# In-projection of three of six chunks: the seven-product scheme applied twice, with 49 products of 128 columns

## The chip, the cores and the metric

The kernel runs on one core of a Trainium2 chip. The metric is the device time of one execution in microseconds. Engines: PE (TensorE, matmuls), PEld (its weight loads), DVE (VectorE), ACT (ScalarE), POOL (GpSimd), SP (SyncE, which issues nearly all DMAs). Each engine runs its own queue in order and waits on semaphores for the others.

## The reference

Attention with a mask by clusters over 4 x 8 heads of 768 tokens, then two projections with a gate between them, on 3072 tokens:

```python
x = attn_out.transpose(0, 2, 1, 3).reshape(B * S, H * D)   # 3072 x 512
h = x @ w_in                                               # w_in 512 x 2048
sp = np.maximum(h, 0.0) + np.log1p(np.exp(-np.abs(h)))     # softplus
g = h * erf(sp)
return (g @ w_out).astype(np.float32)                      # w_out 2048 x 512
```

Everything here is in float32. The change concerns `x @ w_in` and the gate behind it.

## The kernel before

The first 408 us are the attention. Then the 3072 tokens run in six chunks of 512 (`CT`), each an in-projection, a gate and an out-projection.

**The seven-product scheme.** A product of two matrices cut into 2 x 2 blocks is made from seven block products instead of eight, at the price of sums of blocks before (`left_forms`, `right_forms`) and after. `lefts` and `rights` name the seven left and right operands by number: 1, 2 and 3 to 7, some of them blocks as they are, some of them sums (`new[0]`, `new[1]`, `new[2]` and one block that is overwritten).

**In-projection before.** The scheme is applied once: x in two halves of tokens (256 columns, `HT`) and two of rows, w_in in halves of rows and columns. `hidden` (called by `hidden26` for chunks 1 to 5, once for each `lot`) goes over four blocks of 128 hidden columns. `block` makes the seven products in the order 1, 2, 6, 7, 5, 3, 4, each of two matmuls of 128x128 weights by 256 columns in a PSUM bank, and after each product its additions out of PSUM (`fresh`): product 1 is copied by ACT, the others are added by DVE into the tiles `g`. So an in-projection is 2 lots x 4 blocks x 7 products x 2 = 112 matmuls. Between the products, one piece of other work at a time is taken off `aside_work`: the gate of the lot before (softplus and erf on ACT, then products on DVE) and the sums that the out-projection needs. The eight PSUM banks are used in turn.

**Out-projection before.** `project26` has 26 products of four matmuls of 256 columns (`RIGHT`, `LEFT`), with sums of blocks of g on DVE between them (`LEFT_STEPS`, each with the product p behind which it stands), and additions and copies out of PSUM on DVE and ACT (`AFTER`, one product behind). Ten of the right operands are streamed from DRAM into three places (`ring`, `load_stream`), issued by SP after the matmuls that used the place. The last quarter of the gate (lot 1, half 1) is done at its start: `curves` for p = −1, 0, 1, 2 on ACT and four gate products on DVE at p = 4 and 5. In its last four products DVE makes the x sums for the next chunk, and SP loads x two chunks ahead at p = 12.

**Order.** All instructions of PE, DVE, ACT and POOL are kept in the order in which the program gives them (`InOrder`); the order is written out by hand. Tiles come from pools: `gp` (g, four), `actp` (one buffer `a_s` for softplus and erf), `outp` (two, the output), `xp` (two, x). A tile that is asked for again waits until its last reader is done. `extra` are the spare rooms in the tiles that hold the ring.

```python
ORDER = (1, 2, 6, 7, 5, 3, 4)
```

Of the kernel before, what the change touches and what calls it, by code (L numbers as in the profile page):

```python
# [9 lines left out]
F32 = mybir.dt.float32  # L10
# [4 lines left out]
ALU = mybir.AluOpType  # L15
# [4 lines left out]
P = 128  # L20
# [13 lines left out]
CT = 512  # L34
# [76 lines left out]
RING = 3  # L111
KEPT = {0: 10, 5: 11}
HELD = 11


class InOrder:
# [16 lines left out]
def kernel(  # L133
# [494 lines left out]
    def right_forms(engine, b11, b12, b21, b22, new):  # L628

        return [  # L630
            functools.partial(minus_of, new[0], b12, b11, engine),
            functools.partial(minus_of, new[1], b22, new[0], engine),
            functools.partial(minus_of, b12, b22, b12, engine),
            functools.partial(minus_of, new[2], new[1], b21, engine),
        ]
# [4 lines left out]
    def rights(b11, b12, b21, b22, new):  # L640
        return {1: b11, 2: b21, 3: b22, 4: new[2], 5: new[0], 6: new[1], 7: b12}

    def w_in_parts(f, n):
        c1, c2 = slice(f * P, (f + n) * P), slice((HF + f) * P, (HF + f + n) * P)
        return (
            w_in[:, 0:HK, c1], w_in[:, HK:, c1], w_in[:, 0:HK, c2], w_in[:, HK:, c2],
            [more_in[:, i, :, c1] for i in range(3)],
        )

    def x_parts(n):  # L650
        x = x_of[n]
        return (
            x[:, 0:HK, 0:HT], x[:, 0:HK, HT:], x[:, HK:, 0:HT], x[:, HK:, HT:],
            [x_more[:, i] for i in range(3)],
        )
# [149 lines left out]


    ring, extra = [], []
    b_dram = dram.tile([N_STREAM + len(KEPT), P, FG * HM], F32, name="b_dram")

    def w_block(b):  # L810
        lot, h = KAPPA[b // 2]
        f = h * HF + lot * FG
        return w_out[:, f : f + FG, (b % 2) * HM : (b % 2 + 1) * HM]

    def slot(i):
        if i < 6:
            at = HOME[i]
            return more_out[:, at // 2, (at % 2) * FG : (at % 2 + 1) * FG]
        return w_block((4, 7)[i - 6]) if i < 8 else ring[i - 8]

    def flat(t):
        return t.rearrange("p f m -> p (f m)")

    def take_places(n):
        for _ in range(n):
            t = gsp.tile([P, 3, FG, P], F32, name="g_more").rearrange("p a j t -> p (a j t)")
            if len(ring) < RING:
                ring.append(t[:, 0 : FG * HM].rearrange("p (f m) -> p f m", f=FG))
                extra.append(t[:, FG * HM :].rearrange("p (j t) -> p j t", j=FG))
            else:  # L830
                extra.append([t[:, i * HM : (i + 1) * HM] for i in range(3)])

    def place26(x, f):
        if x == HELD:
# [23 lines left out]
    def load_stream(k):  # L858
        nc.sync.dma_start(out=flat(ring[(k + 2) % RING]), in_=b_dram[k % N_STREAM])

    def left26(n, i):
        if i >= 16:
            return extra[i - 16]
        lot, h = KAPPA[i % 4]
        t = i // 4
        return g_of[n, t // 2, lot][:, h, :, (t % 2) * P : (t % 2 + 1) * P]

    def left_step(n, x):
# [4 lines left out]
    def gate26(n, lot, half):  # L873
        gs = [g_of[n, s, lot][:, :, 2 * half : 2 * half + 2].rearrange("p h j t -> p h (j t)") for s in range(2)]
        box = []

        def soft(s):
            if not s:
                box.append(actp.tile([P, 2 * FG * HT], F32, name="a_s"))
            ae.activation(  # L880
                out=box[0][:, s * 1024 : (s + 1) * 1024].rearrange("p (h j) -> p h j", h=2),
                in_=gs[s], func=ACT.Softplus,
            )

        def erf(s):
            t = box[0][:, s * 1024 : (s + 1) * 1024]
            ae.activation(out=t, in_=t, func=ACT.Erf)

        def product(s, h):
            c = slice((2 * s + h) * 512, (2 * s + h + 1) * 512)  # L890
            ve.tensor_tensor(out=gs[s][:, h], in0=box[0][:, c], in1=gs[s][:, h], op=ALU.mult)

        halves = [[functools.partial(f, s) for s in range(2)] for f in (soft, erf)]
        return *halves, [functools.partial(product, s, h) for s in range(2) for h in range(2)]
# [5 lines left out]
    def hidden26(n, lot, generation=()):  # L900
# [23 lines left out]
        for work in generation:  # L924
            work()

    def project26(n):
        for s in range(2):
            osb_of[n, s] = outp.tile([P, 2, DM], F32, name="osb")
        temps = extra[3]  # L930

        def c_at(i):
            if i >= 8:
                return temps[i - 8]
            t = i // 2
            return osb_of[n, t // 2][:, t % 2, (i % 2) * HM : (i % 2 + 1) * HM]

        first_half, second_half, gate_products = gate26(n, 1, 1)
        curves = {-1: first_half[0], 0: first_half[1], 1: second_half[0], 2: second_half[1]}
        gate_products = [gate_products[i] for i in (3, 1, 0, 2)]  # L940
        between = right_forms(ve, *x_parts(n + 1)) if n + 1 < NCHUNK else []
        banks26 = {}

        def evict(p):
            m = banks26.pop(p)
            if n == NCHUNK - 1 and p == len(RIGHT) - 1:
                minus_of(c_at(2), c_at(2), m)
                plus_of(c_at(4), c_at(4), m)
            for op, d, src, sign in AFTER[p] if n < NCHUNK - 1 or p < len(RIGHT) - 1 else ():
                dst = c_at(d)  # L950
                source = m if op in "ca" else c_at(src)
                if op in "aA":
                    (plus_of if sign > 0 else minus_of)(dst, dst, source)
                elif op == "C" and p == 4:
                    if sign > 0:
                        ve.tensor_copy(out=dst, in_=source)
                    else:
                        ve.tensor_scalar(out=dst, in0=source, scalar1=-1.0, scalar2=None, op0=ALU.mult)
                elif sign > 0:
                    ae.copy(out=dst, in_=source)  # L960
                else:
                    ae.activation(out=dst, in_=source, func=ACT.Copy, scale=-1.0)
            for t in range(4):
                parts = [DONE[2 * t], DONE[2 * t + 1]]
                o = osb_of[n, t // 2]
                if n + 1 < NCHUNK:
                    if max(parts) == p:
                        nc.sync.dma_start(out=out_v[2 * n + t // 2, :, t % 2], in_=o[:, t % 2])
                else:
                    for v in range(2):  # L970
                        if parts[v] == p:
                            c = slice(v * HM, (v + 1) * HM)
                            queue = nc.scalar if p == len(RIGHT) - 1 and t == 2 else nc.sync
                            queue.dma_start(out=out_v[2 * n + t // 2, :, t % 2, c], in_=o[:, t % 2, c])

        curves[-1]()
        for p, r in enumerate(RIGHT):
            banks26[p] = m = bank()
            lhs = left26(n, LEFT[p])
            g26 = N_STREAM * (n - 1) + r - 100  # L980
            rhs = ring[(g26 + 2) % RING] if r >= 100 else slot(r) if r >= 0 else w_block(-1 - r)
            for f in range(FG):
                te.matmul(m, lhsT=lhs[:, f], rhs=rhs[:, f], start=(f == 0), stop=(f == FG - 1))
            if r >= 100:
                if g26 + RING < N_STREAM * (NCHUNK - 1):
                    load_stream(g26 + RING)
            for x, step in enumerate(LEFT_STEPS):
                if step[0] == p:
                    left_step(n, x)
            if p < 3:  # L990
                evict(p)
                curves[p]()
            elif p - LAG >= 3:
                evict(p - LAG)
            if p in (4, 5):
                for f in gate_products[(p - 4) * 2 : (p - 4) * 2 + 2]:
                    f()
            if p >= len(RIGHT) - 4 and between:
                between.pop(0)()
            if p == 12:  # L1000
                load_x(n + 2)
        for p in sorted(banks26):
            if n == NCHUNK - 1 and p == len(RIGHT) - 1:
                plus_of(c_at(2), c_at(2), c_at(8))
                minus_of(c_at(4), c_at(4), c_at(8))
            evict(p)
        for s in range(2):
            for lot in range(2):
                del g_of[n, s, lot]
# [265 lines left out]
    making.append(functools.partial(load_kept, 0))  # L1275
    making.append(functools.partial(load_stream, 1))
    for n in range(1, NCHUNK):
        if n > 1:
            hidden26(n, 0)
        hidden26(n, 1, making if n == 1 else ())  # L1280
        project26(n)


# [30 lines left out]
```

## Time and profile before

| | us |
|---|---|
| median of three runs | 978.01 (977.81 to 978.02) |
| profiled execution, first to last instruction | 976.0 |
| attention | 0 to 408 |
| in-projection of each of chunks 2 to 5 | 48.35 |
| out-projection of each of chunks 1 to 5 | 44.9 to 45.1 |

The stages of chunks 2 to 5 begin at 598.81 (in), 647.15 (out), 692.05, 740.39, 785.29, 833.63, 878.52 and 926.87. They are read from the matmuls' operands: x and w_in in an in-projection, g and w_out in an out-projection.

One f32 matmul is two records of MATMUL and two of LDWEIGHTS in the profile. A record's length includes the time through the array, so records overlap; what a stream costs is read from start to start. In the page's strips each digit is the busy tenth of 1/40 of the span:

```profile
PE   8999999999999999999999999999999999999998
...
DVE  8888888888888886879788786568666856685766
ACT  3777777777777665377613430562155235413541
POOL 1688887788888888853199600000000000000000
PEclk9999999999999999999999999999999999999999
DMA  9444444444444211142004543023302320131023
```

### The profile page before, as it was taken

To read this page: it belongs to the slowest core of one execution; us is meant where nothing else is said; L and a number is where in the kernel's file an instruction comes from. 1 tells how busy PE (TensorE), PEld (TensorE's weight loads), DVE (VectorE), ACT (ScalarE), POOL (GpSimd) and SP (SyncE) were. 2 spreads that over 40 slices of the span, in tenths; PEclk is the share of its full clock that TensorE was granted. 3 is DMA by queue.
4 is the path that set the end of the run, shared out by engine and by line. 5 is a ranking of instruction groups with operands and counts; after the bars stand their busy time and mean duration, and the time that the engine had idled before them with its cause. 6 is when DMAs were issued, how large, how long until landed. Compare 5 with 4: busy or idle time off the path is not lost.

```text
span 976.0 us, 20840 instructions
## 1 busy us (share of the span) xinstructions
PE 967.6 (99%) x8282; PEld 723.8 (74%) x8282; DVE 758.8 (78%) x1432; ACT 526.7 (54%) x799; POOL 410.0 (42%) x277
## 2 busy tenths in 40 slices
PE   8999999999999999999999999999999999999998
PEld 3555555555555555688888888888888888888887
DVE  8888888888888886879788786568666856685766
ACT  3777777777777665377613430562155235413541
POOL 1688887788888888853199600000000000000000
PEclk9999999999999999999999999999999999999999
DMA  9444444444444211142004543023302320131023
GB/s 226 74 109 110 108 110 109 107 110 109 87 110 110 54 35 34 50 149 87 0 22 173 194 147 135 1 65 130 108 0 87 130 87 1 65 139 57 1 86 108
DMA packets 157185, 88.42 MB, mean 91 GB/s; under 512 B 129696, under 2 KB 139424, under 8 KB 157088
## 3 DMA queue, kind: packets, MB, share of 16 engines
q1 hardware_dynamic: 154592, 86.67, 31.5%
q8 instruction: 65, 1.06, 0.4%
q10 hardware_dynamic: 2496, 0.43, 0.2%
q14 instruction: 32, 0.26, 0.1%
HBM read 68.19 MB, written 18.87 MB: 89 GB/s over the span
## 4 chain that ended last, share of the span: by engine, by line
PE 97%; DVE 2%; DMA 0%; issue 0%; ACT 0%; DVEq 0%; SPq 0%
PE bank L124 43%; PE turned L124 32%; PE sc L124 17%; PE wide L124 6%; DVE nmx L124 1%; DMA in_q<-in_q_dram 0%; DVE kT L124 0%; DVE sims L124 0%; DVE qT L124 0%; DVE km L124 0%; DVE turned L124 0%; DVE nbig L124 0%; ACT qm L124 0%; DVE ccT L124 0%; DVE osb L124 0%
## 5 line engine op out<-in xcount | busy, mean ns | idle before, releaser
L124 POOL TENSOR_TENSOR more_out<-more_out,pr 128x768 f32<-128x768 f32 x128 | 217.2, 1697 | 18.5 <-ACT pr L124 10.0
L124 DVE TENSOR_REDUCE nmx<-wide 128x2 f32<-128x768 f32 x189 | 180.5, 955 | 47.8 <-PE wide L124 47.0
L124 ACT ACTIVATE pr<-sc 128x768 f32<-128x768 f32 x192 | 148.7, 810 | 94.1 <-PE wide L124 77.2
L124 PE MATMUL turned<-pr,in_v 128*32 128x193 f32 x3072 | 144.8, 330 | 0.0
L124 DVE TENSOR_TENSOR g<-bank,g 128x256 f32<-128x256 f32 x222 | 89.4, 419 | 54.2 <-PE bank L124 34.1
L124 PEld LDWEIGHTS turned<-pr,in_v 128*32 128x32 f32 x3072 | 91.5, 109 | 50.7 <-issue 21.3
L124 DVE TENSOR_TENSOR g<-g 128x512 f32<-128x512 f32 x114 | 78.9, 692 | 42.3 <-PE bank L124 32.2
L124 PE MATMUL bank<-x_own,w_in 128*128 128x256 f32 x424 | 104.5, 379 | 0.0
L124 PE MATMUL sc<-qT,kT 64*128 64x384 f32 x528 | 98.3, 486 | 0.0
L124 PEld LDWEIGHTS bank<-x_own,w_in 128*128 128x128 f32 x424 | 80.4, 190 | 11.5 <-issue 0.6
L124 ACT ACT_TABLE_LOAD x48 | 61.6, 1283 | 38.2 <-DVE g L124 37.5
L124 DVE TENSOR_TENSOR g<-a_s,g 128x512 f32<-128x512 f32 x96 | 74.1, 786 | 3.2 <-ACT a_s L124 3.2
L124 PE MATMUL bank<-x_more,more_in 128*128 128x256 f32 x296 | 76.0, 379 | 0.0
L124 PE MATMUL bank<-w_out,g 128*128 128x256 f32 x328 | 75.7, 379 | 0.0
L124 POOL TENSOR_TENSOR more_out<-pr,pr 128x768 f32<-128x768 f32 x32 | 60.3, 1886 | 28.3 <-ACT pr L124 28.3
L124 PE MATMUL bank<-g_more,g 128*128 128x256 f32 x296 | 69.9, 379 | 0.0
L124 PEld LDWEIGHTS bank<-w_out,g 128*128 128x128 f32 x328 | 62.2, 190 | 8.6
L124 PEld LDWEIGHTS <-qv 64*128 64x128 bf16 x384 | 27.0, 93 | 52.9 <-issue 36.7
L124 PEld LDWEIGHTS sc<-qT,kT 64*128 64x128 f32 x528 | 50.0, 187 | 21.4 <-ACT inv L124 2.4
L124 PE MATMUL wide<-kv,qv 64*128 64x384 bf16 x378 | 64.0, 328 | 1.3 <-DVE nmx L124 0.6
L124 PE MATMUL wide<-km,qm 64*128 64x384 bf16 (+1 forms) x378 | 62.6, 327 | 0.0
L124 PEld LDWEIGHTS bank<-g_more,g 128*128 128x128 f32 x296 | 56.2, 190 | 7.6
(195 smaller groups left out, 1745.6 us busy)
## 6 DMA issues: line engine op xcount, KB each, us to landing
g_more<-b_dram SPq DMA_DIRECT2D x48, 512.0 KB, 3.2
x_own<-in_moe_w_in_dram SPq DMA_DIRECT2D x13, 512.0 KB, 4.1
in_v<-in_v_dram SPq DMA_DIRECT2D x32, 192.0 KB, 3.1
x_dram<-more_out SPq DMA_DIRECT2D x128, 48.0 KB, 1.8
x_own<-x_dram SPq DMA_DIRECT2D x6, 1024.0 KB, 5.5
in_k<-in_k_dram SPq DMA_DIRECT2D x59, 96.0 KB, 2.6
in_q<-in_q_dram SPq DMA_DIRECT2D x58, 96.0 KB, 2.6
out_dram<-osb SPq DMA_DIRECT2D x20, 256.0 KB, 3.2
```

Of the source, the lines that this page charges most:

```text
L124: ins = getattr(self.engine, name)(*args, **kw)
```

## The change

For chunks 3, 4 and 5 (`TWICE = 3`) the in-projection is `hidden49`: the scheme is applied to blocks of blocks. There are 7 x 7 = 49 products, each of four matmuls (one for each of four blocks of hidden columns, which stand side by side in one bank) of 128x128 weights by 128 columns of x: 196 matmuls. `SLOTS` gives their order: i is the number of the product in the inner scheme, o in the outer, in three groups of i: (1, 2), (6, 7, 4), (5, 3).

- **Sums in PSUM.** o = 1 begins a bank (`chain`) that 6, 7 and 4 then add to; o = 5 begins another (`second`) that 3 adds to; o = 2 has a bank of its own. Before a bank is added to again, its present value is copied (ACT, o = 1, 5, 6) or used (DVE, `feed`, o = 2, 7, 3; `feed_last`, o = 4). The copies are kept in `extra` and the two output tiles until they are needed. The further sums between blocks of g are done by POOL (`ge_onto`).
- **Weight forms.** Three of the seven weight forms of the inner scheme (i = 4, 5, 6; 21 blocks of 256 KB) are made once by POOL, before chunk 2's in-projection (`forms_twice`), and stored in DRAM (`w_dram`). In each of the three chunks they are loaded again (`load_twice`) into halves of the ring's tiles, six of them ahead of need. The fourth (i = 7) is made in place by seven POOL operations behind chunk 2's in-projection (`last_form_twice`).
- **x forms** of the inner scheme: eight DVE operations in slots 0 to 5 (`x_twice`).
- **Gate.** Of the 16 gate products of a chunk, eight are done in the in-projection (`gate_early`, at the slots in `also`) and eight at the start of the out-projection (`soft_late`, `gate_after`), where four were before.
- **Loads.** x of the next chunk is loaded at the start of the out-projection for chunks 4 and 5, and the last uses of the ring are followed by loads of weight forms.

```diff
+GROUPS = (((1, 2), (1, 5, 6, 3, 7, 2, 4)), ((6, 7, 4), (1, 2, 5, 6, 3, 7, 4)), ((5, 3), (1, 5, 6, 3, 7, 2, 4)))
+SLOTS = [(i, o) for inner, outer in GROUPS for o in outer for i in inner]
+STREAMED = [s for s in SLOTS if s[0] in (4, 5, 6)]
...
+    def forms_twice():
...
+            for i, form, a, b in ((5, minus_of, b12, b11), (6, minus_of, b22, new[0]), (4, minus_of, new[1], b21)):
+                t = new[{5: 0, 6: 1, 4: 2}[i]]
+                form(t, a, b, ge)
+                nc.sync.dma_start(out=w_dram[STREAMED.index((i, o))], in_=t)
+    def last_form_twice():
+        for o in STEPS:
+            w = lefts(*w_in_parts(0, HF))[o]
+            b12, b22 = (w[:, k, FG * P :] for k in range(2))
+            minus_of(b12, b22, b12, ge)
...
+    def soft_late(n, s):
+        if s:
+            t = actp.tile([P, 2 * FG * HT], F32, name="a_s")
+        else:
+            t = x_extra[n].rearrange("p k t -> p (k t)")
+        for tt in (1, 0) if s else (0, 1):
+            curves_of[n, s, tt] = c = t[:, tt * 1024 : (tt + 1) * 1024]
+            ae.activation(out=c, in_=quarter(n, s, 1, tt), func=ACT.Softplus)
...
+        soft_late(n, 0)
+        curves = {0: [erf(1, 1)], 1: [erf(0, 0)], 2: [erf(0, 1), erf(1, 0)]}
+        products_at = {3: [12], 4: [0, 7], 5: [11, 15], 6: [3, 8], 7: [4]}
...
+        def copied(i, which, m):
+            t = held[i, which] = fixed[i, which] if (i, which) in fixed else temps.pop(0)
+            ae.copy(out=t, in_=m)
+            if i == 3:
+                ge_onto(gs(WHERE[which])[1], t)
+        def feed(i, which, m):
+            g11, g12, g21, g22 = gs(WHERE[which])
+            if i == 3:
+                onto(g12, m)
+                return
+            t = held.pop((i, which))
+            dst = {1: g12, 2: g11, 7: g22, 4: g21}.get(i, t)
+            plus_of(dst, m, t)
+            if i == 2:
+                ge_onto(g11, g12)
+            elif i == 6:
+                ge_onto(g12, t)
+            elif i == 7:
+                ge_onto(g22, g12)
+            elif i == 4:
+                minus_of(g21, g22, g21, ge)
+            elif i == 5:
+                ge_onto(g22, t)
+                ge_onto(g12, t)
+            if (i, which) not in fixed:
+                temps.append(t)
...
+        also = {
+            0: x_forms[0:2], 1: x_forms[2:3], 2: x_forms[3:4], 3: x_forms[4:6], 4: x_forms[6:7], 5: x_forms[7:8],
+            10: [soft1[1]], 14: [soft1[0]], 15: [erf1[1]], 16: [erf1[0]],
+            20: products1[0:1], 21: products1[1:2], 22: products1[2:3], 23: products1[3:4],
+            33: [soft2[1]], 36: [soft2[0]], 37: first_steps[0:1], 38: first_steps[1:2], 40: [erf2[1], erf2[0]],
+            43: products2[0:1], 44: products2[1:2], 45: products2[2:3] + first_steps[2:], 46: products2[3:4],
+            47: [functools.partial(soft_late, n, 1)],
+        }
+        for at, (i, o) in enumerate(SLOTS):
+            w, x = w_twice(n, i, o), x_form(i, o)
+            if o in (1, 2, 5):
+                m = free.pop(0)
+                if o != 2:
+                    (chain if o == 1 else second)[i] = m
+            else:
+                m = (second if o == 3 else chain)[i]
+            for j in range(FG):
+                te.matmul(
+                    m[:, j * P : (j + 1) * P], lhsT=w[:, j * P : (j + 1) * P], rhs=x,
+                    start=(o in (1, 2, 5) and j == 0), stop=(j == FG - 1), skip_group_check=True,
+                )
...
+            if o in (1, 5, 6):
+                copied(i, {1: "x", 5: "w", 6: "u"}[o], m)
+            elif o == 4:
+                feed_last(i, m)
+            else:
+                feed(i, {2: "x", 7: "w", 3: "u"}[o], m)
+            if o in (2, 3, 4):
+                free.append(m)
+            for f in also.get(at, ()):
+                f()
...
-        curves[-1]()
+        for f in curves.get(-1, ()) if n >= TWICE else [curves[-1]]:
+            f()
...
-            if p in (4, 5):
-                for f in gate_products[(p - 4) * 2 : (p - 4) * 2 + 2]:
-                    f()
+            for f in products_at.get(p, ()):
+                f()
...
     for n in range(1, NCHUNK):
-        if n > 1:
-            hidden26(n, 0)
-        hidden26(n, 1, making if n == 1 else ())
+        if n + 1 == TWICE:
+            forms_twice()
+        if n >= TWICE:
+            hidden49(n)
+        else:
+            if n > 1:
+                hidden26(n, 0)
+            hidden26(n, 1, making if n == 1 else ())
+        if n + 1 == TWICE:
+            last_form_twice()
         project26(n)
```

In the names below, (i,w), (i,u) and (i,x) stand for `feed(i, which, m)` of product i: x belongs to o = 2, u to o = 3 and w to o = 7. In the last group the slots are 35, 36 (o = 1; i = 5, 3), 37, 38 (o = 5), 39, 40 (o = 6), 41, 42 (o = 3), 43, 44 (o = 7), 45, 46 (o = 2), 47, 48 (o = 4).

## Prediction

> **What bounds the kernel now.** I read the page first: who is busy, and what the chain that ended last is made of.
>
> ```profile
> PE 967.6 (99%) x8282; PEld 723.8 (74%) x8282; DVE 758.8 (78%) x1432; ACT 526.7 (54%) x799; POOL 410.0 (42%) x277
> ...
> PE 97%; DVE 2%; DMA 0%; issue 0%; ACT 0%; DVEq 0%; SPq 0%
> ```
>
> TensorE is the chain from end to end. Then the busy time by stage, cut where the matmuls change from in-projection to out-projection (chunks 2 and 3 here; 4 and 5 repeat them):
>
> ```profile
> 598.81:647.15 48.34, 48.34 (x225) 42.56 (x224) 30.62 (x73) 22.37 (x26) 0.00 (x0) 1.00 0.08 28
> 647.15:692.05 44.90, 44.90 (x210) 39.52 (x209) 34.27 (x72) 15.14 (x30) 0.00 (x0) 1.00 0.40 135
> 692.05:740.39 48.34, 48.34 (x225) 42.56 (x224) 30.61 (x73) 22.37 (x26) 0.00 (x0) 1.00 0.08 28
> 740.39:785.29 44.90, 44.90 (x210) 39.52 (x209) 34.27 (x72) 15.14 (x30) 0.00 (x0) 1.00 0.40 135
> ```
>
> Columns: stretch, length, busy PE, weight loads, DVE, ACT, POOL, then granted clock, DMA share, GB/s. PE has no gap and a full clock. An in-projection is 112 f32 matmuls, two records each: 48.34 / 224 = 215.8 ns a record of 256 columns. DVE has 17 us free in an in-projection and 10 in an out-projection, POOL all of it. Last, the timeline where a weight load was late, and the groups that the new work resembles (first two of the last fence: 600 to 971 us, POOL idle; others: 495 to 552 us, POOL running):
>
> ```profile
> 408.07 0.19 PEld L124 LDWEIGHTS bank<-x_own,w_in 128*128 128x128 f32 x1 [0.31 <-issue]
> 408.07 0.48 PE L124 MATMUL bank<-x_own,w_in 128*128 128x256 f32 x1
> ...
> 408.18 0.41 PEld L124 LDWEIGHTS bank<-x_own,w_in 128*128 128x128 f32 x2
> ```
>
> ```profile
> L124 DVE TENSOR_TENSOR g<-bank,g 128x256 f32<-128x256 f32 x144 | 58.4, 420 | 46.7 <-PE bank L124 29.1 <-ACT g L124 15.3
> L124 DVE TENSOR_TENSOR g<-a_s,g 128x512 f32<-128x512 f32 x64 | 42.9, 681 | 0.0
> ...
> L124 DVE TENSOR_TENSOR g<-a_s,g 128x512 f32<-128x512 f32 x13 | 17.4, 1359 | 1.1 <-ACT a_s L124 1.1
> L124 DVE TENSOR_TENSOR g<-bank,g 128x256 f32<-128x256 f32 x26 | 10.3, 417 | 2.4 <-PE bank L124 1.6
> ...
> L124 POOL TENSOR_TENSOR more_out<-w_out,more_out 128x512 f32<-128x512 f32 x6 | 9.3, 1562 | 0.0
> L124 POOL TENSOR_TENSOR g_more<-w_out,more_out 128x512 f32<-128x512 f32 x3 | 3.8, 1265 | 0.0
> ```
>
> An add with both inputs in SBUF doubles beside POOL (681 to 1359), and POOL's goes from 1265 to 1562 on average; an add that reads PSUM stays (420, 417).
>
> **Part 1, the matmuls (chunks 3 to 5): −5.5 us each.** 112 matmuls of 256 columns become 49 x 4 = 196 of 128, 392 records. No row has this shape. Streaming alone: a 256-column record costs 215.8 = two passes at 0.4167 ns a column (213.3) + 2.5; with 128, 109.2. Loading alone: at 408.07 the load and its matmul are stamped together and that matmul lasts 0.48 instead of 0.379, so it began 104 ns late; the next load starts at 408.18, again as the matmul gets going. A load thus takes some 107 ns and goes under the matmul before it: 109 again. The far end is the load's record, 0.19, if nothing of it overlapped: 190. I take 109.3, the late loads being the same operation: 392 x 109.3 = 42.85 against 48.35. At 190 it would be +31.6 a chunk.
>
> The Trainium skill (TensorE: Matmul & The Clock Gate, "Back-to-back issue gap") speaks against it: streams of load and matmul pairs sustain 81 ns at 128 columns where an isolated matmul needs 56. Added as 25 ns to each record, an estimate from that page, that is 9.8 us a chunk and some 29 us in all. The late loads above show no such addition, and the sum goes without it.
>
> **Part 2, adds that move to POOL, and who waits for them: +4.2 us in each of the three in-projections.** Start to start in the timeline, where two of a kind follow each other, a DVE add takes 0.33 at 256 and 0.60 at 512, an ACT operation 0.25 at 256 and 0.95 at 1024, a POOL add of 512 1.25. So per chunk: 28 PSUM adds of 512 on DVE at 0.60, 22 copies on ACT at 0.48 (between its two rows), 21 SBUF adds on POOL at 1.25. In sum all fit; the order doesn't. A product is 0.874 us, slot s ends at 0.874(s+1), a reader starts 0.2 us later. In slots 26 to 31 six POOL adds are released from 24.5 on and end at 32.0. The softplus put into ACT's queue at slot 33 waits for the last; behind it stand the copies of slots 35 and 36, done at 33.8. From there POOL owes seven adds in a row before product (3,w) can be stored: x at 35.1; w at 37.0 (its copy stands behind the second softplus); u at 38.2; the pair of (5,u) at 40.7. DVE, in order, stands at the add of (3,u) until then: 41.4, and only then reaches (5,w): 42.0. POOL's next pair 44.5, and 0.45 more for each of two gate products that DVE runs beside it: 45.4; DVE's add of (3,w): 46.1. Slot 48 accumulates into the bank that this add reads, and was due at 41.95: 4.2 late. With the copies in time and no sharing the same walk gives 44.8, 2.9 late; with the early left steps also beside POOL about 5.0.
>
> **Part 3, the gate that is left for the out-projection: +3.8 us, three times.** Where the in-projection ends (E), DVE still has two products, two adds and a step to do, and behind them waits for POOL's pair of (5,x), E+3.3. Its last gate product ends at E+4.6, and only that frees the one a_s buffer, for which ACT's table load waits. Then ACT: load 1.29, four softplus of 0.95, a copy 0.25, load 1.29, erf 0.95: E+12.3. Now DVE can go on: product 12 and the step of p=4 end at E+13.6, but PE's eighth product wants that step at E+7x1.727 = 12.1. Behind it DVE has seven products, three steps and four adds (7.3 us) until the step that p=10 needs, E+20.9; p=10 is due at 17.3: 3.6 late, and some tenths later. I take 3.8. If DVE weren't behind at E, the chain would end 3.1 earlier and cost 0.4; at worst, by the sharing above, 4.6. Before, this place holds one 5.7 us chain of ACT (two softplus, four products) and PE never stops.
>
> **Part 4, the forms made once: +4.0 us.** 21 POOL forms and 21 stores of 256 KB run in chunk 2's in-projection: twelve gate products there cost DVE 0.7 more each, 8 of its 17 free us; zero. If that cover fails, 2. The seven last forms must wait for the last in-projection matmul, so they lie at the start of the out-projection, beside DVE's four products and three steps: 7 x 0.7 = 4.9 later, on the queue that ACT's table load waits for. I take 4.0 of it; bounds 0 (all in DVE's 10 free us) and 5.2.
>
> **Moved or added at nothing.** The x forms (eight DVE adds) stand in slots 0 to 5, where DVE has no PSUM add; else 4.3. Six table loads a chunk instead of eight: ACT is off the path there. 21 loads of 256 KB a chunk: after six that are fetched ahead, 3.9 MB in slots 14 to 48, 128 GB/s, where 135 is moved in an out-projection at a DMA share of 0.40; at half of that they'd cost some 30 us a chunk. In SP's queue the first of these loads stand ahead of the last two output stores (0.4 us each); the copies that wait for those stores have 1 us to spare. Fewer bank waits: PE has none now.
>
> **Sum.** 3 x (−5.5 + 4.2 + 3.8) + 4.0 = +11.5. The profiled span is 976.0, the median of the runs 978.0, 2.0 more around it: 978.0 + 11.5 = 989.5. Extremes of the terms: 3 x (−5.5 + 2.9 + 0.4) + 0 = −6.6, and 3 x (−5.5 + 5.0 + 4.6) + 5.2 + 2 = +19.5, to which 6 ns more a record add 7.
>
> **Rivals.**
> - The adds keep pace (other side). Parts 2 and 3 are bounds of queues at measured rates; if POOL's adds overlap better (1.25 are spacings between free-running ones), only the matmuls count: 978.0 − 16.5 = 961.5, or 971 at the low extreme. For it: all four queues fit in sum (POOL 26 of 43 us). Against it: PE accumulates in banks that DVE must read first, and DVE is in order. It decides if both waits together stay under 5.5 a chunk.
> - Weight loads become the bound. At 190 ns 978.0 + 3 x 31.6 = 1073; the queues would then hide. For it: the rows of 256 columns never test a load every 109 ns. Against: 408.07.
> - The streamed forms come late. PE would wait on a DMA in slots 14 to 34; at 110 GB/s, as in much of the first half, 3.9 MB need 35.7 us instead of 30.6: +5 a chunk, about 1000 with part of the other waits covered.
> - It balances: waits of 5.5 a chunk and nothing in chunk 2: 978.
>
> **How the numbers follow.** Forecast (PE waits for DVE and POOL) 0.70; adds keep pace 0.13; loads 0.05; late forms 0.06; balance 0.06. Predicted 989.5, its own range 983 to 997. From 979 to 1001 leaves out the fast rival and the slow loads. Under 0.2% (2 us) is what a measurement can't tell from no change: faster 0.13, same 0.06, slower 0.81.
>
> **What would show it.** Right: matmul records of 128 columns 109 ns apart; in-projections of 46 to 48 us whose only gaps lie in the last slots, ended by DVE, with DVE idle there on POOL; out-projections of 48 to 49.5, with a gap at the eighth to eleventh product. Wrong: in-projections of 43; or even spacing above 112; or PE waits that a DMA ends.

## The result and the profile after

The kernel after takes 994.5 us (median of 4 runs, 993.3 to 994.82) where the kernel before took 978.01 in the same session (977.81 to 978.03): a ratio of 1.0168, 95% interval 1.0153 to 1.0182. It is slower, by 16.5 us. The profiled execution of after spans 992.7 us against 976.0, so the traces have 16.7 us to explain.

The first two lines are from the page of after: busy time by engine, and the chain that ended last, by engine.

```profile
PE 964.9 (97%) x8786; PEld 731.5 (74%) x8786; DVE 780.3 (79%) x1372; ACT 545.8 (55%) x835; POOL 532.3 (54%) x368
...
PE 89%; ACT 4%; DVE 3%; POOL 2%; issue 1%; DMA 1%; POOLq 0%; DVEq 0%; ACTq 0%; SPq 0%
```

TensorE was 97% of the chain and is 89%; the rest now passes through ScalarE, VectorE and GpSimd. DMA has 1%, none of it in chunks 3 to 5. PE's busy time hardly fell, although some 14 us of matmul time were taken out (4.6 a chunk, below): part of that is matmuls at half clock, below. Then the busy time by stage of after, with the cuts where the matmuls change (columns: stretch, length, busy PE, weight loads, DVE, ACT, POOL, then granted clock, DMA share, GB/s):

```profile
598.90:647.25 48.35, 48.35 (x226) 42.56 (x225) 30.35 (x67) 22.38 (x26) 31.11 (x24) 1.00 0.38 142
647.25:695.71 48.46, 45.37 (x210) 39.35 (x208) 40.24 (x77) 15.06 (x30) 7.29 (x5) 1.00 0.31 104
695.71:743.97 48.26, 44.53 (x393) 44.15 (x392) 29.47 (x45) 24.90 (x34) 24.66 (x19) 1.00 0.51 164
743.97:793.46 49.49, 47.45 (x209) 40.18 (x209) 40.31 (x79) 18.85 (x34) 3.31 (x2) 0.97 0.30 100
793.46:842.45 48.99, 45.26 (x394) 44.87 (x392) 30.50 (x46) 24.98 (x34) 25.32 (x20) 0.97 0.51 164
842.45:891.23 48.78, 47.43 (x210) 40.45 (x210) 39.88 (x78) 18.85 (x34) 2.67 (x2) 0.96 0.31 103
```

The first line is chunk 2's in-projection, with full PE. The second is its out-projection: 3.1 us without PE. From the third on come chunks 3 and 4 in the new scheme: every in-projection holds 392 records and some 44 us of matmuls, yet lasts as long as the old one, and every out-projection has grown. In us, all stages from the traces, with those of the experiments to come:

| | in 2 | out 2 | in 3 | out 3 | in 4 | out 4 | in 5 | out 5 and end |
|---|---|---|---|---|---|---|---|---|
| before | 48.35 | 44.89 | 48.35 | 44.89 | 48.35 | 44.89 | 48.35 | 49.08 |
| after | 48.35 | 48.46 | 48.26 | 49.49 | 48.99 | 48.78 | 48.99 | 52.49 |
| e1 | 48.35 | 47.22 | 44.27 | 49.41 | 44.28 | 49.43 | 44.27 | 53.14 |
| e2 | 48.35 | 48.88 | 48.97 | 48.77 | 48.97 | 48.77 | 48.08 | 53.35 |
| e3 | 48.35 | 49.10 | 49.41 | 47.07 | 49.42 | 47.07 | 49.12 | 51.09 |
| e4 | 48.35 | 48.46 | 43.85 | 46.63 | 43.85 | 46.63 | 43.84 | 50.34 |
| e5 | 48.35 | 44.89 | 48.39 | 49.34 | 48.98 | 48.75 | 48.98 | 52.48 |
| e6 | 48.35 | 45.78 | 51.13 | 49.20 | 48.97 | 48.77 | 48.98 | 52.49 |
| e7 | 48.35 | 44.89 | 51.61 | 48.77 | 49.00 | 48.77 | 48.51 | 52.97 |
| e8 | 48.35 | 44.89 | 48.27 | 46.27 | 46.01 | 46.27 | 46.01 | 49.97 |
| e9 | 48.35 | 46.77 | 46.15 | 46.43 | 46.50 | 46.05 | 46.00 | 49.98 |
| e10 | 48.35 | 47.22 | 46.01 | 46.58 | 46.28 | 46.31 | 46.64 | 49.63 |

The 16.7 us are 3.6 in chunk 2's out-projection, 1.2 in the three in-projections together (−0.1, +0.6, +0.6) and 11.9 in the three out-projections (+4.6, +3.9, +3.4).

Where chunk 3's in-projection ends and its out-projection begins, the timeline of after reads as follows (columns: start, length, engine, line, operation, out<-in, shapes, how many, and in brackets the idle time before it with its releaser):

```profile
735.27 2.50 POOL L130 TENSOR_TENSOR g<-g,osb 128x512 f32<-128x512 f32 x2
...
737.81 0.69 DVE L130 TENSOR_TENSOR g<-bank,g 128x512 f32<-128x512 f32 x1 [3.54 <-POOL g L130]
738.41 0.68 DVE L130 TENSOR_TENSOR osb<-bank,osb 128x512 f32<-128x512 f32 x1
739.01 0.68 DVE L130 TENSOR_TENSOR g<-a_s,g 128x512 f32<-128x512 f32 x1
...
739.15 1.16 PE L130 MATMUL bank<-x_own,g_more 128*128 128x128 f32 x8 [1.22 <-DVE osb L130]
739.17 2.86 POOL L130 TENSOR_TENSOR g<-g,osb 128x512 f32<-128x512 f32 x2 [1.40 <-DVE osb L130]
742.07 0.69 DVE L130 TENSOR_TENSOR g<-turned,g 128x512 f32<-128x512 f32 x1 [2.38 <-POOL g L130]
...
742.82 1.36 PE L130 MATMUL turned<-g_more,w_in 128*128 128x128 f32 x8 [2.51 <-DVE g L130]
...
747.99 0.68 DVE L130 TENSOR_TENSOR g<-a_s,g 128x512 f32<-128x512 f32 x1
...
748.77 1.28 ACT L130 ACT_TABLE_LOAD   x1 [11.74 <-DVE g L130]
...
750.07 2.01 ACT L130 ACTIVATE a_s<-g 128x1024 f32<-128x1024 f32 x2
...
754.24 1.28 ACT L130 ACT_TABLE_LOAD   x1
755.54 1.06 ACT L130 ACTIVATE a_s<-a_s 128x1024 f32<-128x1024 f32 x1
...
756.63 0.69 DVE L130 TENSOR_TENSOR g<-a_s,g 128x512 f32<-128x512 f32 x1 [4.63 <-ACT a_s L130]
...
757.98 0.48 PE L130 MATMUL turned<-more_out,g 128*128 128x256 f32 x1 [0.23 <-DVE g L130]
```

Read it from the brackets. VectorE stands 3.54 us before 737.81, until GpSimd's pair of adds is done, then makes two adds, the second of which frees a bank; PE's product of slot 47 starts at 739.15, 1.4 us late. GpSimd's next pair can only start now; VectorE stands again (2.38), and the product of slot 48 starts at 742.82, another 2.7 us late. VectorE's last gate product starts at 747.99, and only that releases ScalarE, idle for 11.74 us: a table load, four softplus, a table load, an erf, and VectorE goes on at 756.63. PE's wait at 757.98 is the first of three.

There is one thing here that no term of the forecast had: the clock. The busy time in stretches of 2 us of after, same columns as above:

```profile
741.00:743.00 2.00, 0.18 (x1) 0.18 (x2) 0.93 (x2) 0.00 (x0) 1.04 (x1) 1.00 0.74 260
743.00:745.00 2.00, 2.00 (x11) 1.82 (x12) 2.00 (x4) 0.00 (x0) 0.96 (x1) 0.66 0.01 2
745.00:747.00 2.00, 2.00 (x7) 1.55 (x6) 1.23 (x1) 0.00 (x0) 2.00 (x2) 0.50 0.00 0
747.00:749.00 2.00, 2.00 (x11) 1.77 (x10) 1.61 (x3) 0.23 (x1) 0.35 (x1) 0.99 0.00 0
```

After the two waits the granted clock (third column from the right) falls to half for 3.4 us; records of 256 columns are 427 ns apart there instead of 216. It happens at the same place in chunk 4, for 6.8 us, and in chunk 5, for 3.4.

### The profile page after: what moved, and what is told of

The parts are those of the page before. It is cut to its first block, busy times and chain, and to the rows that moved or that the text cites. A ratio compares the mean times of both kernels' runs of the same rounds, so it can differ in the third digit from the quotient of the medians.

```text
span 992.7 us, 22118 instructions
## 1 busy us (share of the span) xinstructions
PE 964.9 (97%) x8786; PEld 731.5 (74%) x8786; DVE 780.3 (79%) x1372; ACT 545.8 (55%) x835; POOL 532.3 (54%) x368
## 4 chain that ended last, share of the span: by engine, by line
PE 89%; ACT 4%; DVE 3%; POOL 2%; issue 1%; DMA 1%; POOLq 0%; DVEq 0%; ACTq 0%; SPq 0%
PE bank L130 38%; PE turned L130 29%; PE sc L130 16%; PE wide L130 6%; POOL g L130 2%; ACT a_s L130 1%; ACT x_own L130 1%; DVE nmx L130 1%; ACT L130 1%; DVE osb L130 1%; DVE g L130 1%; ACT g_more L130 0%; ACT osb L130 0%; DMA g_more<-b_dram 0%; DVE g_more L130 0%
## 5 line engine op out<-in xcount | busy, mean ns | idle before, releaser
L130 POOL TENSOR_TENSOR g<-g 128x512 f32<-128x512 f32 x27 | 35.4, 1311 | 162.4 <-DVE g L130 161.0
L130 DVE TENSOR_TENSOR g<-bank,g 128x256 f32<-128x256 f32 (+1 forms) x133 | 58.6, 457 | 38.1 <-POOL g L130 13.0
L130 PE MATMUL bank<-g_more,g 128*128 128x256 f32 x336 | 79.8, 380 | 3.5 <-ACT g_more L130 3.5
L130 PE MATMUL bank<-x_own,w_in 128*128 128x256 f32 (+1 forms) x416 | 77.5, 327 | 0.0
L130 PEld LDWEIGHTS bank<-g_more,g 128*128 128x128 f32 x336 | 63.3, 190 | 13.9 <-ACT g_more L130 4.7
L130 PE MATMUL bank<-w_out,g 128*128 128x256 f32 x296 | 69.3, 380 | 0.0
L130 PEld LDWEIGHTS bank<-x_own,w_in 128*128 128x128 f32 x416 | 64.2, 191 | 6.0 <-issue 0.6
L130 ACT ACTIVATE a_s<-g 128x1024 f32<-128x1024 f32 (+1 forms) x38 | 42.7, 1146 | 37.6 <-POOL g L130 34.6
```

Source lines behind the costliest of these rows:

```text
L130: ins = getattr(self.engine, name)(*args, **kw)
```

## The experiments

The times of e1 to e7 are one run each, beside 977.88 (e1 to e4) and 977.78 (e5 to e7) of the kernel before on the same chip; those of e8 to e10 are medians of ten or eleven runs.

**e1: the GpSimd add of the fifth product into the second sum is put off.** In `feed`, it leaves the pair and stands after the PSUM add of the third.

```diff
             if i == 3:
                 onto(g12, m)
+                ge_onto(g12, fixed[5, which])
                 return
...
             elif i == 5:
                 ge_onto(g22, t)
-                ge_onto(g12, t)
```

> Same work on every engine; POOL's add of product (5,.) into g12 stands behind DVE's add of product (3,.) instead of ahead of it. If DVE's place in the queue is what PE waits for: the rewritten in-projections fall from 48.3 to 49.0 us to 44.2 to 44.8 (392 records of 111.7 ns and some tenths for late copies), the granted clock is 1.00 in them, the out-projections stay at 48.5 to 50, total 980 to 984. If the amount of work is too large for DVE and POOL, or the port that they share: in-projections stay above 47, total 990 or more. If ACT's late copies hold PE: in-projections about 46 to 47.

It took 980.82. The windows of e1 for chunk 3:

```profile
694.30:738.57 44.27, 44.11 (x393) 43.91 (x392) 30.33 (x44) 24.86 (x34) 23.99 (x19) 1.00 0.52 168
738.57:787.99 49.42, 46.01 (x211) 39.03 (x210) 41.60 (x81) 18.82 (x34) 4.47 (x3) 1.00 0.34 112
```

POOL makes the same adds as in after, only in another order (28.5 us of them in the two stages, against 28.0), and the in-projection is 44.27 instead of 48.26. So it isn't the amount of GpSimd work that stalls PE, but its place ahead of adds that VectorE, in order, needs. The out-projection stays at 49.4, with a full clock: its loss has another cause.

**e2: the seven last forms are written down behind chunk 3's slots 0 to 6.**

```diff
-        if n + 1 == TWICE:
-            last_form_twice()
...
+            if n == TWICE and at in (0, 1, 2, 3, 4, 5, 6):
+                last_form_twice(GROUPS[1][1][(0, 1, 2, 3, 4, 5, 6).index(at)])
```

> The seven last weight forms move from the start of chunk 2's out-projection to slots 0 to 6 of chunk 3's in-projection. If they cost the 3.6 us of that out-projection (part 4 of the prediction): it falls from 48.5 to 45 to 46, total 991 to 992.5. If the 21 forms of the in-projection before it cost it (costed at nothing): it stays above 47, total 993 or more. Chunk 3's in-projection may gain up to 1 us, since the x forms on DVE share slots 0 to 5 with them.

It took 995.0, and chunk 2's out-projection 48.88. The timeline of e2, GpSimd alone, shows why this tells nothing:

```profile
642.11 2.50 POOL L130 TENSOR_TENSOR w_in<-w_in 128x512 f32<-128x512 f32 x2 [9.01 <-PE bank L130]
645.57 4.17 POOL L130 TENSOR_TENSOR more_in<-more_in 128x512 f32<-128x512 f32 x3 [0.95 <-PE bank L130]
649.70 3.40 POOL L130 TENSOR_TENSOR w_in<-w_in 128x512 f32<-128x512 f32 x2
```

The forms ran when they did in after (641.9 to 654.6), since nothing else stood in GpSimd's queue: a later place in an empty queue is not a later time. e6 does it with a dependency.

**e3: the gate products come earlier.** Two in slot 43 and two in slot 44, instead of one each in slots 43 to 46.

```diff
-            43: products2[0:1], 44: products2[1:2], 45: products2[2:3] + first_steps[2:], 46: products2[3:4],
+            43: products2[0:2], 44: products2[2:4], 45: first_steps[2:],
```

> The last four early gate products stand two slots earlier in DVE's queue (slots 43 and 44 instead of 43 to 46). If the chain of part 3 holds (last product, a_s buffer free, ACT's table load, four softplus, erf, product 12): the out-projections of chunks 3 to 5 fall from 48.8 to 49.5 to 47 to 48, in-projections within 0.5 of before, total 989 to 992. If DVE has simply too much to do in the out-projection: out-projections stay within 0.5, total 993 or more.

It took 991.01. Windows of e3 for chunk 3:

```profile
696.08:745.50 49.42, 45.24 (x394) 44.86 (x392) 31.86 (x47) 25.49 (x35) 25.12 (x20) 0.97 0.49 160
745.50:792.57 47.07, 47.07 (x210) 40.59 (x209) 37.91 (x77) 18.30 (x34) 2.83 (x2) 0.96 0.31 105
```

The table load comes at 744.87, before the in-projection's end, instead of 4.8 us after it, and the out-projection falls from 49.49 to 47.07; the clock is half in its first microseconds, and PE has no gap left. The in-projection pays more than the 0.5 that was expected: 49.42, for the products now stand ahead of the add that frees the last bank. The chain from the gate product through ScalarE is thus what the out-projection waits for.

**e4: the six GpSimd adds of the fifth product are left out of each of chunks 3 to 5.** The sums lack that product.

```diff
             elif i == 5:
-                ge_onto(g22, t)
-                ge_onto(g12, t)
+                pass
```

> Leaves out the two POOL adds of each product (5,x), (5,w) and (5,u): six of 21 POOL adds a chunk, so g lacks these terms. If the wait for them is parts 2 and 3 nearly whole: in-projections 44.2 to 44.8, out-projections 46 to 47.5, clock 1.00, total 972 to 977. If something else holds PE in the last slots (late copies, the port): in-projections stay at 46 or more, total 983 or more.

It took 972.58. The window of e4 for chunk 3's in-projection:

```profile
695.73:739.58 43.85, 43.85 (x394) 43.85 (x393) 29.92 (x46) 24.86 (x34) 19.33 (x15) 1.00 0.50 168
```

The in-projections are 43.85 with no PE gap, the sum of 392 records and nothing else, and the out-projections 46.63. This is the size of the gain that the scheme has in its in-projection when nothing waits: 4.5 us a chunk.

**e5 to e7: which forms cost chunk 2 its 3.6 us?** In e5, 18 of the 21 forms made in chunk 2's in-projection are left out (the three that are made are stored again and again, and chunks 3 to 5 run on them). In e6 all forms are made, but the seven last ones stand behind GpSimd adds of chunk 3 that depend on its matmuls. e7 does both, and lacks the same 18 forms.

```diff
e5, e7
-            new = [places[(n + i) % 4] for i in range(3)]
-            n += 3
+            new = places[:3]
+            n += 1
...
-                form(t, a, b, ge)
+                if n == 1:
+                    form(t, a, b, ge)
...
e6, e7
+            if n == TWICE:
+                for o in {9: (1, 2), 11: (5, 6, 3), 19: (7, 4)}.get(at, ()):
+                    last_form_twice(o)
```

> Of the 21 weight forms that GpSimd makes in chunk 2's in-projection, 18 are left out (the 21 stores stay, and chunks 3 to 5 run on three of the forms, repeated, as weights); the seven last forms stay where they are. My theory now, from the trace of after: the 21 forms double the time of four gate products of chunk 2's in-projection (1.09 to 1.44 us instead of 0.68), so that ScalarE's gates start 2.6 us late (627.1 instead of 624.5, 639.1 instead of 636.5), and this is about half of what chunk 2's out-projection loses: it comes down from 48.46 to 45.6-46.4 us and the time from 994.5 to 991.4-993. Rival, the forecast as I made it (these forms cost nothing, the seven last forms cost all of the 3.57): chunk 2's out-projection stays at 48.2-48.7 and the time at 994-995. All stages of chunks 3 to 5 within 0.3 of after under both.

> The seven last forms are moved to chunk 3's in-projection, and this time behind GpSimd adds that depend on matmuls of slots 6 to 18, so that they can't start early. The 21 forms stay. My theory (each set of forms makes about half of the 3.57): chunk 2's out-projection 48.46 -> 45.8-46.8 us. Rival (the last forms make all of it): 44.9-45.2. Second rival (they make none, the late gates alone do): 48.2 or more. In chunk 3's in-projection the seven adds (9 us of GpSimd) now stand in the queue whose backlog ends it: 48.26 -> 49-50.5. Sum: 993.3 to 994.8 under my theory.

> Both edits together: 18 of the 21 forms left out (chunks 3 to 5 run on three of the forms, repeated), and the seven last ones held back to chunk 3's in-projection. My theory (chunk 2's out-projection loses its time to these two sets of adds and to nothing else): 44.9-45.2 us, as before the change, and chunk 3's in-projection 49-50.5 as in the run with the last forms held alone; time 991.8-993.3. Rival (something else is late in chunk 2, say the stores or the loads of the streamed forms, which stay): 45.8 or more.

They took 991.18, 993.81 and 993.75. Chunk 2's out-projection: 44.89 in e5, 45.78 in e6, 44.89 in e7. e5 fell below what my theory allowed: the 18 forms alone took the whole 3.6 away. e6 ended at the foot of its range, and in both runs with held forms chunk 3 paid more than I had written, 51.1 and 51.6. What all this means is read from when ScalarE can load the table for the last gate of chunk 2. Its lines in the timelines of before, after, e5 and e6 (ScalarE alone), in this order:

```profile
648.52 1.28 ACT L124 ACT_TABLE_LOAD   x1 [5.12 <-DVE g L124]
```

```profile
653.82 1.28 ACT L130 ACT_TABLE_LOAD   x1 [7.83 <-DVE g L130]
```

```profile
649.87 1.28 ACT L130 ACT_TABLE_LOAD   x1 [6.28 <-DVE g L130]
```

```profile
650.70 1.28 ACT L130 ACT_TABLE_LOAD   x1 [5.12 <-DVE g L130]
```

Counted from the start of the out-projection, the load comes at 1.37 us in before, 2.53 in e5, 3.91 in e6 and 6.57 in after, and the stage loses 0, 0, 0.89 and 3.57. The loss is the load's time less 3.0: TensorE has 1.6 us of slack, and what goes beyond costs its full length. The same rule holds in e7 (1.37: 0), e8 (3.01: 0), e9 (4.89: 1.88), e10 (5.34: 2.33), e1 (5.35: 2.33) and e4 (6.58: 3.57); e2 and e3, with a half clock in this stage, are 0.4 and 0.6 above it. e7 keeps all stores and loads of the forms and loses nothing, so these are not the cause. And neither set of forms is to blame by itself. The last forms alone hide, the 21 forms alone cost 0.9, and together they cost 2.3 to 4.2 in the five runs that make both as after does (after, e1 to e4).

The gate products of chunk 2 show why the sum is more than its parts. The 21 forms slow the four products of an earlier gate, to 1.44, 1.43, 1.09 and 1.42 us. Three of them in the timeline of after:

```profile
620.22 1.44 DVE L130 TENSOR_TENSOR g<-a_s,g 128x512 f32<-128x512 f32 x1
...
623.93 1.09 DVE L130 TENSOR_TENSOR g<-a_s,g 128x512 f32<-128x512 f32 x1
...
625.28 1.42 DVE L130 TENSOR_TENSOR g<-a_s,g 128x512 f32<-128x512 f32 x1
```

In before each takes 0.68, and ScalarE's next gate starts 2.5 us earlier. In e5 that gate is in time, and only the last two of its four products run beside the last forms (1.10 and 1.42): 1.2 us of lateness. In e6 it is 2.5 late and meets no forms. In after it is 2.5 late and for that reason all four products meet the last forms (1.48, 1.42, 1.10 and 1.42): 2.5 + 2.7 = 5.2, the whole delay of the table load. e1's chunk 2 has the same instructions as after and lost 2.3 instead of 3.6, since the first product of each of the two gates took 0.79 and 0.93 instead of 1.44 and 1.48: which adds meet is a matter of tenths of a microsecond, and a single run's value for this stage is good to about 1 us.

**e8: all computed, the queues shortened.** Besides e1's edit: for w the put-off add, and for x the add of the third product, are VectorE's; the products stand in slots 43 and 44 (and two of the first half's, and one erf, a slot away from where they were); the 21 forms come in lots of 12, 3 and 6, each behind a gate product of chunk 2; the last forms are held as in e6.

```diff
-                ge_onto(gs(WHERE[which])[1], t)
+                add(ve if which == "x" else ge, gs(WHERE[which])[1], t)
...
+                add(ve if which == "w" else ge, g12, fixed[5, which])
...
+            43: products2[0:2], 44: products2[2:4],
+            47: [functools.partial(soft_late, n, 1)], 48: first_steps[2:],
```

> A version with the whole computation that takes the measured causes together: the GpSimd add of 5 into g12 waits for slot 3's PSUM add and is made by VectorE for w, as is that of (3,x); the gate products of the second half stand at slots 43 and 44, the last first-step at 48; the 21 forms are made in three lots, each behind a gate product of chunk 2; the seven last forms are held back to chunk 3. My theory (all loss comes from the order of VectorE's, ScalarE's and GpSimd's queues): in-projections of 4 and 5 at 44.7-45.8 us, out-projections 45.5-47.3, chunk 2's out-projection 44.9-46, granted clock 0.998 or more; time 971-978, so at or below the 978.0 before. Rival (the scheme's extra adds can't be covered at all in an out-projection of 44.9): out-projections stay at 48.5-49.5 as in the run that only deferred the adds, time 981 or more.

It took 977.36 (10 runs) against 977.78: ratio 0.9996, interval 0.9987 to 1.0006, no difference. The expected time range held; the in-projections of chunks 4 and 5 came out 0.2 us above theirs. The granted clock, expected at 0.998 or more, was lower in six of the ten executions: these took 977.27 to 977.72, the other four 976.68 to 976.91. What is left in these in-projections is this, in the timeline of e8:

```profile
827.60 3.45 DVE L130 TENSOR_TENSOR g<-a_s,g 128x512 f32<-128x512 f32 x2
...
830.97 0.68 DVE L130 TENSOR_TENSOR g<-turned,g 128x512 f32<-128x512 f32 x1
...
831.70 0.41 PEld L130 LDWEIGHTS turned<-g_more,w_in 128*128 128x128 f32 x3 [2.08 <-DVE g L130]
```

Two gate products take 1.7 us each beside GpSimd's adds instead of 0.68, and the add that frees the last bank stands behind them.

**e9 and e10: the last forms back in chunk 2.** e9 is e8 without the held forms; in e10 the lots of the 21 forms are 12, 6 and 3.

```diff
e9
-            if n == TWICE:
-                for o in {9: (1, 2), 11: (5, 6, 3), 19: (7, 4)}.get(at, ()):
-                    last_form_twice(o)
...
e10
-            if o in (7, 2):
+            if o in (7, 4):
                 yield
```

> The version of the run before with one edit: the seven last forms are back at the start of chunk 2's out-projection, as in the kernel after; the three fenced lots of the 21 forms and the shorter queues stay. My theory, from the runs with one set of forms away: the seven last forms cost nothing in chunk 2's out-projection as long as ScalarE's gates start there in time, and held back to chunk 3 they cost its in-projection 48.27 - 46.01 = 2.26 us. So chunk 2's out-projection 44.9-45.7, chunk 3's in-projection 45.9-46.2, time 975.0-976.2 against 977.36, ratio to before 0.9972-0.9984: faster than before by 0.2 to 0.3%. Rival (the fences delay the lots into the last forms, so that the two sets meet again, as in the kernel after): chunk 2's out-projection 47-48.5, time 977.3-978.8, no gain over before.

> The version of the run before with one edit: of the 21 forms, the lot behind the first gate has 6 and the lot behind the second has 3, instead of 3 and 6, so that the last lot is done (636.6 + 3 x 1.4 = 640.8 us) before the seven last forms can start at 641.9. My theory, from the table loads of the last gate in chunk 2 (648.5 before, 649.9 with the last forms alone, 650.7 with the 21 forms alone, 651.7 in the run before, 653.8 in the kernel after) and from what each cost (0, 0, 0.89, 1.88, 3.57): TensorE gives some 1.7 us of slack, and only what is later than that is lost. Here the load should come at 650.0-650.6, chunk 2's out-projection at 44.9-45.7 us (46.77 in the run before), time 974.5-975.5, ratio to before 0.9965-0.9976. Rival (the six forms of the earlier lot slow the next four gate products instead, so that the lateness only changes its place): load at 651.5 or later, out-projection 46.5 or more, time 976.3 or more.

e9 took 976.44 (11 runs) against 977.9: ratio 0.9987, interval 0.9978 to 0.9996. e10 took 975.89 (11 runs) against 977.87: ratio 0.9981, interval 0.9972 to 0.9990. Chunk 3's in-projection fell from 48.27 to 46.15 and 46.01, as expected; chunk 2's out-projection rose to 46.77 and 47.22, which I had not expected in either. ScalarE's line in the timeline of e10:

```profile
652.64 1.28 ACT L130 ACT_TABLE_LOAD   x1 [8.00 <-DVE g L130]
```

I had put the load at 650.0 to 650.6; the rival had 651.5 or later. Its numbers for the load and the stage came out, its reason did not. In e9 and e10 alike the middle lot slows one product of an earlier gate (1.57 instead of 0.68), with three forms or with six, and the last forms slow all four of the last gate (1.59, 1.42, 1.09, 1.42 in e9; 1.66, 1.42, 1.09, 1.42 in e10). What e10's load is later by is the first product of the earlier gate, 1.05 beside the end of the lot of twelve. e10 has the lowest median with the whole computation, but its interval overlaps that of e9, and its gain of 2.0 us over before is no larger than the 0.2% that counts here as a difference.

## Why the prediction was right, and where its sizes were off

The forecast, that PE waits for VectorE and GpSimd and that these waits exceed the shorter matmuls, held: 994.5 lies in the range, 5.0 above the predicted 989.5. By span, 16.7 were found where 11.5 were summed.

- **Part 1, the matmuls.** Streams of 128 columns run at 111.66 ns a record (in chunks 3 to 5, 762 spacings of 112 and 380 of 111), where 109.3 was taken. e4's stage confirms it: 392 x 111.66 = 43.8, measured 43.85. The gain is 4.6 us a chunk, not 5.5; over three chunks the sum was 2.8 too low. Why a record of 128 columns takes 2.4 ns more than the forecast had isn't shown. The addition of 25 ns a record that I weighed from the Trainium skill (TensorE: Matmul & The Clock Gate, "Back-to-back issue gap") would have meant an in-projection 9.8 us longer; no stage shows it.
- **Part 2, 4.2 us at the end of each in-projection.** Measured 1.38 + 2.68 = 4.06 in chunk 3, behind the adds that the walk named: the larger part at slot 48, as it had it, the smaller already at slot 47. e1 and e4 show the cause from two sides: the same adds in another order, and six adds less, both take the stall away.
- **The clock, in no part, and not on the path here.** After that stall the matmuls run at half clock. In chunks 4 and 5 this makes the in-projection 0.7 us longer than in chunk 3. But chunk 4's out-projection is 0.7 shorter than chunk 3's, and the two stages together take 97.75 and 97.77 us. The chain that ended last, around the half clock of chunk 3, has no matmul from 738.0 to 763.75:

```profile
737.04 0.91 PE turned L130 x8
...
744.04 3.32 POOL g L130 x2
...
763.75 6.35 PE bank L130 x27
```

  In this stretch GpSimd, VectorE and ScalarE set the time, and a slower PE only waits less later. e1's out-projection, at full clock, is as long (49.41).
- **Part 3, 3.8 us in each out-projection.** Measured +4.6, +3.9 and +3.4, 11.9 against 11.4. The times of the chain fit to some tenths: from the end of the in-projection (E = 743.97) the last gate product ends at E + 4.7 (4.6 foretold), the first erf is out at E + 12.6 (12.3), PE's wait at its eighth product lasts until E + 14.0. The last and longest wait, 1.4 us, is at the tenth product and ends with a copy by ScalarE at E + 19.1; the walk had it at the eleventh, ended by a step of VectorE at E + 20.9. e3 showed that an earlier start of this chain shortens it, e1 that it doesn't depend on the stall before it.
- **Part 4, 4.0 us in chunk 2, measured 3.6.** The sum is right and its working is not. The step that failed is "twelve gate products there cost DVE 0.7 more each, 8 of its 17 free us; zero": four of them were slowed (1.09 to 1.44 us instead of 0.68), and that made ScalarE's gates 2.5 us late, although VectorE had free time. The charge of the seven last forms, 4.0 of 4.9, failed with it: alone they make the table load 1.2 us later and cost nothing (e5), since PE has 1.6 us of slack there. The fallback price for the 21 forms, 2, was kept out of the sum and was what the other term covered by chance.
- **The sum.** Of the 5.2 us that were missing, part 1 is 2.8. Parts 2 and 3 together are another 2.8: in- and out-projection lose 9.1, 9.1 and 8.6 us in chunks 3, 4 and 5, where 8.0 was summed. Part 4 is 0.4 the other way.
- **At nothing, rightly.** The loads of the forms: DMA share 0.51 and 164 GB/s in the in-projection, more than the 128 needed, and no wait of PE in chunks 3 to 5 that a DMA ended. Six table loads instead of eight: no effect seen. The x forms in slots 0 to 5: no gap in these slots.
- **The rivals.** Adds that keep pace (961.5, or 971 at the low extreme) is what e4 comes near to, by leaving adds out. Even e10, with the queues in a better order, is at 976: the scheme's in-projection gains 1.7 to 2.3 us a chunk, and the work that is left at its end costs the out-projection 0.6 to 1.7 of that, chunk 2 another 2.3. The price of the slow loads was reckoned wrongly: 31.6 a chunk is counted from the 42.85 forecast; counted from the 48.35 before, 190 ns a record is 26.1 a chunk, which makes 1056 and not 1073.

What stays open: how fast the version with neither the 2.06 us wait in the last slots nor the lateness in chunk 2 would be; it wasn't tried.

## What to carry to other kernels

When work moves to engines that are half idle, walk their queues in order at the place where TensorE needs a bank or a step; a sum of busy times says only that the work fits somewhere. Price two sets of small delays on the same chain together, against its slack: here one was free, one cost 0.9 and both cost 2.3 to 4.2. And to move an operation in time, tie it to something that happens then.

## What the hardware showed that I had not expected

- **After a wait of 2 us TensorE's clock is sometimes half, and sometimes not.** In e8 and e10 the same wait of 2.06 us stands near the end of each in-projection. After it the clock stays full in e8, and in e10 it is half (the windows are below). In the profiled run of e10, which was the slowest of its eleven (977.71; the fastest 975.38; that of e8 was the fastest of its ten), it follows that wait in all three chunks, for some 3.4 us each; in e9 in chunks 3 and 4 and not in chunk 5. It costs less than the 1.7 us it takes from PE: in e10 in-projection 4 is 0.27 longer with it than in e8, and out-projection 4 is 46.31 against 46.27, because PE would have waited 1.27 us there later.

  What decides is where the wait lies. In all twelve traces the recorded clock keeps one value for a whole number of steps of 3.41 us, until the last change at the kernel's end. Cut into these steps, from 598 us on, 26 steps at full clock hold 2.05 us or more of PE's waits (those over 0.3 us), and after 25 of them the clock is half; after none of the 80 that hold 0.5 to 1.77 us. The one exception is e9's chunk 5, where the wait ends 0.02 us before its step does. Two steps of e10, then two of e8:

```profile
829.43:832.84 3.41, 1.50 (x14) 1.31 (x13) 3.38 (x5) 0.00 (x0) 1.50 (x1) 1.00 0.84 234
832.84:836.25 3.41, 3.41 (x12) 2.87 (x11) 3.41 (x6) 2.12 (x2) 1.55 (x2) 0.50 0.18 72
```

```profile
826.95:830.36 3.41, 2.87 (x26) 2.67 (x24) 3.41 (x4) 1.07 (x2) 3.41 (x3) 1.00 0.39 121
830.36:833.77 3.41, 2.07 (x13) 1.95 (x14) 3.38 (x6) 0.09 (x1) 0.14 (x1) 1.00 0.66 205
```

  In e10 the whole wait lies in one step; in e8 a step's end cuts it into 0.71 and 1.34 us, and the clock stays full. That the wait in one step is the cause is read from this count; no run was made to test it.
- **How much VectorE and GpSimd slow each other varies from one operation to the next.** The forecast had means. Here a VectorE product of two SBUF inputs, 0.68 us alone, took up to 1.78 where GpSimd adds ran beside it, and such an add, 1.27 alone, up to 1.73.
